# Two cached attention decodes on one core: the order of the first loads, and when the second problem's queries are made

## The chip, the cores and the metric

The kernel runs on one core of one Trainium2 chip. The metric is the device time of one execution in microseconds, the median of several runs. Five engines work side by side, each with an instruction stream of its own: TensorE (PE, with its weight loads shown apart as PEld), VectorE (DVE), ScalarE (ACT), GpSimd (POOL) and SyncE (SP). SP computes nothing here; it issues nearly all loads. Streams meet only at semaphores: an instruction waits until another engine, or a transfer that lands, has counted a semaphore up to a value. An engine that waits holds up everything behind it in its own stream.

## The reference

Two independent problems A and B of the same shape are computed, each one step of multi-head attention against a stored cache, and their results stand side by side:

```python
# B, Sq, D = 8, 1, 1024;  H, Sk, Dh = 32, 4096, 128;  bfloat16
q = (x @ wq).reshape(B, Sq, H, Dh).transpose(0, 2, 1, 3)
scores = einsum("bhqd,bhkd->bhqk", q, k_cache) * Dh ** -0.5
p = softmax(scores, axis=-1)
o = einsum("bhqk,bhkd->bhqd", p, v_cache)
result = o.transpose(0, 2, 1, 3).reshape(B, Sq, H * Dh) @ wo
```

Every batch row and head has keys and values of its own, 1 MB each, and they are used once. All of them have to come from memory: 2 x 2 x 8 x 32 MB and the weights.

## The kernel before, in words

**Slots.** The work is cut into 64 slots (`NS`), numbered n: problem c, group g of eight heads, batch row b. A slot's keys are one load of 8 MB (8.39 million bytes) into 128 partitions, 16 partitions to a head and 256 keys to a partition; its values are another of the same size. `kbuf` has two places for keys, used in turn (`k0`, `k1`); `vbuf` has one place for values (`v`). Below, K0, K1 and so on are the key loads, and V0, V1 and so on the value loads, of slots 0, 1 and so on.

**One slot.** `multiply` (line 354, DVE) multiplies a quarter of the keys with the slot's query in place, in `kbuf`; `add_up` (line 364, PE) sums the products over parts of the head dimension into the banks `red`; `reduce` (line 376, DVE) finishes the sums into the scores in `osb`. This happens four times, and the last `add_up` sets the key place free. `softmax` (lines 381 to 385, DVE) finds the maxima, `exps` (line 392, ACT) makes the eight heads' exponentials into `prob` and their row sums. `rowsum` (line 398, PE) and `invert` (line 404, DVE) make the reciprocals of the row sums. The product with the values, `pv` (line 415, PE), is done one slot later: slot n does `pv(n-1)` behind its last `add_up`, which sets `vbuf` free. `copy_o`, `gather` and `heads` bring the results into place; now and then `permute` and `project` multiply them with a part of the output weights, with `asb`, `osum` and `orow` as the places of the projection.

**Order.** `Program.add` records every operation with what it reads and writes by name, and puts it at the end of its engine's stream. `finish` turns these names into semaphore waits. A load into a place waits, on SP, for the last reader of that place. So the streams have exactly the order in which the Python code calls `add`. In slot n (line 542 on) the call order on SP is: `load_k(n)`, sometimes a load of output weights, `load_v(n-1)`. So V(n-1) and K(n+1) are issued right behind each other, when `pv(n-2)` is done in slot n-1. Slots from 1 on run in hardware loops on PE, ACT and DVE.

**The start.** Before slot 0 the queries are made. `load_wq` (line 251) loads the query weights of a problem, 8 MB like a key load: A's into `vbuf`, B's into the second key place, one behind the other. `make_xT` (line 257) transposes the inputs x, which ACT's queue has loaded, and puts them into a part of `prob` (`xT`). `make_q` (line 267) has three steps: 64 matmuls with 512 columns each (line 273, PE), in groups of four that stand side by side in the array, into the banks `oacc` and `late`; two casts to bfloat16 (line 278, DVE) into another part of `prob` (`qrow`); and 32 small matmuls that turn the rows into columns (line 284, PE), with a copy into `qT` (line 288, DVE). `pick_q(0)` (line 335, POOL) and `make_qbc(0)` (lines 342 and 346, PE and ACT) then spread the queries of slots 0 and 1 over the partitions, into `qbc`; they need A's queries alone. The sequence is A's weights, B's weights, K0 on SP without a wait; then K1, which goes into the place of B's weights and so waits for B's `make_q` matmuls; then V0, whose place A's matmuls have left.

Of the kernel before, what the change touches and what calls it, by code (L numbers as in the profile page):

```python
# [8 lines left out]
BF16 = mybir.dt.bfloat16  # L9
# [134 lines left out]
def _build(nc, caches, out):  # L144
    x0, k0, v0, wq0, wo0 = caches[0]
    B, Sq, D = x0.shape
    _, H, Sk, Dh = k0.shape
    NC = len(caches)
# [7 lines left out]
    R = D // 128  # L156
# [9 lines left out]
    with es:  # L166
# [8 lines left out]
        kbuf = sb("kbuf", [128, 2, T * Dh], BF16)  # L175
        vbuf = sb("vbuf", [128, T * Dh], BF16)
        wob = sb("wob", [128, 2, D], BF16)
        prob = sb("prob", [128, T, HP], BF16)
        osb = sb("osb", [128, TB * Dh], FP32)
        asb = sb("asb", [128, CW], FP32)  # L180
        osum = sb("osum", [128, CW], FP32)
        orow = sb("orow", [128, CW], BF16)
        qT = sb("qT", [128, NC, H * B], BF16)
        qbc = sb("qbc", [128, 2, Dh], BF16)
        ident = sb("ident", [128, 128], BF16)
# [15 lines left out]
        score = osb[:, 0:T]  # L201
        olate = asb[:, 0:2 * Dh]
        xs = wob[:].rearrange("p a n -> p (a n)").rearrange("p (c n) -> p c n", c=NC)
        flat = prob[:].rearrange("p t h -> p (t h)")
        xT = flat[:, 0:NC * R * B].rearrange("p (c r b) -> p c r b", c=NC, r=R)
        qrow = flat[:, 1024:2048].rearrange("p (k n) -> p k n", k=2)
        otail = kbuf[:, 1, 0:2 * TB * Dh].bitcast(FP32)
        wlast = vbuf[:, 0:HP * D].rearrange("p (h n) -> p h n", h=HP)

# [1 line left out]
        oacc = ps("oacc", [128, 512])  # L211
        late = ps("late", [128, 512])
        acc = ps("acc", [128, 512])
        bps = ps("bps", [128, 512])
        sps = ps("sps", [128, 512])
        qps = [(oacc, "oacc"), (late, "late")]
# [6 lines left out]
        def dma(eng, dst, src, writes, sem, reads=()):  # L223
            return P.add(eng, lambda e: e.dma_start(dst, src), reads=reads, writes=writes, dma=sem)  # L224
# [24 lines left out]
                op.sig = True  # L249

        def load_wq(c):
            dst = (vbuf[:], kbuf[:, 1, :])[c]
            name = ("v", "k1")[c]
            dma("sp", dst, caches[c][3].rearrange("(p r) n -> p (r n)", r=R), [name], name)
            return name, dst.rearrange("p (r n) -> p r n", r=R)

        def make_xT(c):
            def emit(e):
                last = None
                for r in range(R):  # L260
                    last = e.matmul(sps[:, 256 + r * B:256 + (r + 1) * B], xs[0:B, c, r::R], ident[0:B, 0:B], start=True, stop=True)
                return last
            P.add("pe", emit, reads=[f"xs{c}", "wo", "ident"], banks=["sps"])
            P.add("dve", lambda e: e.tensor_copy(xT[:, c].rearrange("p r b -> p (r b)"), sps[:, 256:256 + R * B]),
                  reads=probs, writes=[f"xT{c}"], banks=["sps"])

        def make_q(c, name, w):
            def emit(e):
                last = None
                for r in range(R):  # L270
                    for k in range(8):
                        q = k % 4
                        last = e.matmul(qps[k // 4][0][32 * q:32 * q + B, :], xT[:, c, r, :], w[:, r, k * 512:(k + 1) * 512],  # L273
                                        start=(r == 0), stop=(r == R - 1), tile_position=(0, 32 * q))
                return last
            P.add("pe", emit, reads=[name, f"xT{c}"] + probs, banks=["oacc", "late"])
            for k in range(2):
                P.add("dve", lambda e, k=k: e.tensor_copy(qrow[:, k, :], qps[k][0][:]), reads=probs, writes=[f"qrow{k}"], banks=[qps[k][1]])  # L278

            def turn(e):  # L280
                last = None
                for h in range(H):
                    q, k = (h // 4) % 4, h // 16
                    last = e.matmul(bps[:, h * B:(h + 1) * B], qrow[:, k, (h % 4) * Dh:(h % 4 + 1) * Dh],
                                    ident[:, 32 * q:32 * q + B], start=True, stop=True)
                return last
            P.add("pe", turn, reads=["qrow0", "qrow1", "ident"] + probs, banks=["bps"])
            P.add("dve", lambda e: e.tensor_copy(qT[:, c, :], bps[:, 0:H * B]), writes=[f"qT{c}"], banks=["bps"])

        def source(c, what, b, g):  # L290
# [7 lines left out]
        def load_k(n):  # L298
            c, g, b = where(n)
            dma("sp", kbuf[:, n % 2, :], source(c, 1, b, g), [f"k{n % 2}"], f"k{n % 2}")  # L300
# [31 lines left out]
        def pick_q(n):  # L332
            c, g, b = where(n)
            src = qT[:, c, g * HP * B:(g + 1) * HP * B].rearrange("p (h b) -> p b h", b=B)[:, b:b + 2, :]
            P.add("pool", lambda e: e.tensor_copy(qg[:], src.unsqueeze(3).to_broadcast([128, 2, HP, SEG])),
                  reads=[f"qT{c}"], writes=["qg"])

        def make_qbc(n):
            def emit(e):
                last = None  # L340
                for j in range(2):
                    last = e.matmul(bps[:, j * Dh:(j + 1) * Dh], qg[:, j].rearrange("p h s -> p (h s)"), ident[:],  # L342
                                    start=True, stop=True)
                return last
            P.add("pe", emit, reads=["qg", "ident"], banks=["bps"])
            P.add("act", lambda e: e.activation(qbc[:].rearrange("p i d -> p (i d)"), bps[:, 0:2 * Dh], ACTF.Copy),  # L346
                  writes=["qbc"], banks=["bps"])
# [31 lines left out]
        def softmax(n):  # L379
            i = n % 2  # L380
            P.add("dve", lambda e: e.tensor_reduce(rmax[:], score, AX.X, ALU.max), reads=scores, writes=["rmax"])  # L381
            P.add("dve", lambda e: e.transpose(tmax[:], rmax[:].to_broadcast([128, 32])), reads=["rmax"], writes=["tmax"])  # L382
            P.add("dve", lambda e: e.tensor_reduce(nmax[:], tmax[:].rearrange("p (s k) -> p s k", s=2), AX.X, ALU.max),
                  reads=["tmax"], writes=["nmax"])
            P.add("dve", lambda e: e.scalar_tensor_tensor(
                bias[:].rearrange("p (k s) -> p k s", s=2), nmax[:].unsqueeze(1).to_broadcast([128, HP // 2, 2]), -scale,
                neg[:].rearrange("p (k s) -> p k s", s=2), ALU.mult, ALU.add), reads=["nmax", "neg"], writes=["bias"])
# [139 lines left out]
        NS = NC * NG * B  # L527
        L0, L1, L2 = 1, B + 1, NS - 1
        vplace = {}
        first = [load_wq(c) for c in range(NC)]  # L530
        for c in range(NC):
            make_xT(c)
        for c, (name, w) in enumerate(first):
            make_q(c, name, w)
            if c == 0:
                pick_q(0)
                make_qbc(0)

        def marks():
            return {e: len(P.order[e]) for e in ("pe", "act", "dve")}  # L540
# [1 line left out]
        for n in range(NS):  # L542
            m = n - 1
            p = (n - B - 2) // 2 if n >= B + 2 and n % 2 == 0 else NP * (NC * NG - 1) - 1 if n == NS - 1 else None
            if n in (L1, L2):
                for e, at in marks().items():
                    P.loops[e].append((start[e], at, (n - was) // 2))
            if n in (L0, L1):
                start, was = marks(), n
            load_k(n)  # L550
            if p is not None:
                load_wo(p)
                pick_heads(p)
            if m >= 0:
                load_v(m)
            if n % 2 == 1 and n + 1 < NS:
                pick_q(n + 1)
            multiply(n, 0)
            if n >= 1:
                heads(n - 2)  # L560
                invert(n - 1)
            add_up(n, 0)
            multiply(n, 1)
            if p is not None:
                permute()
            reduce(n, 0)
            if p is not None:
                permuted()
            add_up(n, 1)
            multiply(n, 2)  # L570
            if p is not None:
                project()
            reduce(n, 1)
            add_up(n, 2)
            multiply(n, 3)
            reduce(n, 2)
            if p is not None:
                projected(p)
            add_up(n, 3)
            reduce(n, 3)  # L580
            softmax(n)
            if m >= 0:
                pv(m)
            if n % 2 == 1 and n + 1 < NS:
                make_qbc(n + 1)
            if n == NS - 1:
                load_v(n)
                load_wo_last()
            exps(n)
            if m >= 0:  # L590
                copy_o(m)
                if n == NS - 1:
                    idle(3)
                gather(m)
            if n == NS - 1:
                heads(m)
                idle(36)
            rowsum(n)
            if n == B * NG + B + 4:
                store(0)  # L600
# [112 lines left out]
```

## Time and profile before

| what | value |
|---|---|
| median of three runs | 2571.3 us (2571.07 to 2572.44) |
| span of the profiled execution | 2570.6 us |
| busy: PE | 1472.9 us (57%) |
| busy: DVE | 1372.3 us (53%) |
| busy: ACT | 647.2 us (25%) |
| busy: POOL | 314.9 us (12%) |
| SP's main DMA queue | 1107.33 MB, 99.8% of 16 engines' span |
| chain that ended last | DMA 33%, PE 23%, DVE 20%, unknown queue 13%, issue 9% |

How to read it. The shares of the engines are busy time over the span; the DMA row counts the time that the queue's packets took, as a share of the time of 16 DMA engines. The page divides the span into 40 slices of 64 us, and gives what the DMA moved in each. The chain is followed back from the last instruction, at each step to what released it. "Unknown queue" stands for waits that end with a landing that the profile does not put to a line. In a timeline each row has its start, its duration, engine, line, operation, and the tile written and read; in brackets the idle time of the engine just before it and what ended that. Queue rows (SPq) show when a load was issued; the time to landing is given apart.

### The profile page before, as it was taken

What the parts mean: (1) busy time and instruction counts of PE and PEld (TensorE: products, weight loads), DVE (VectorE), ACT (ScalarE), POOL (GpSimd) and SP (SyncE); (2) the same over time, 40 slices, a digit from 0 to 9 for tenths busy, and PEclk for the clock granted to TensorE, in tenths of its full rate; (3) what the DMA queues carried; (4) which work ended last, traced back from release to release, by engine and by line L of the source; (5) the groups of instructions that cost most, each with busy time, mean ns of one, the idle gap of its engine ahead of it and who ended that gap; (6) DMA issues with size and microseconds to landing.
All of it is one profiled execution on the core that took longest, in us unless ns stands there. A gap on an engine that the chain in (4) does not pass through costs nothing.

```text
span 2570.6 us, 19444 instructions
## 1 busy us (share of the span) xinstructions
PE 1472.9 (57%) x9528; PEld 290.3 (11%) x5688; DVE 1372.3 (53%) x969; ACT 647.2 (25%) x1121; POOL 314.9 (12%) x166
## 2 busy tenths in 40 slices
PE   2565565565555655655656656556555565565566
PEld 1011111011111111010111111110101111111102
DVE  1755465465564554645645545546456455465463
ACT  0223313313223123132132231331322322313313
POOL 0011011011011110110111101101101111011010
PEclk7877787877877878878778778787787787787888
DMA  9999999999999999999999999999999999999999
GB/s 424 393 439 426 440 433 435 432 430 432 432 433 432 436 434 432 432 432 428 440 433 432 432 432 430 432 432 435 435 432 434 432 433 433 432 435 432 432 432 391
DMA packets 24446, 1107.55 MB, mean 431 GB/s; under 512 B 2720, under 2 KB 2784, under 8 KB 7408
## 3 DMA queue, kind: packets, MB, share of 16 engines
q1 hardware_dynamic: 24368, 1107.33, 99.8%
q8 instruction: 8, 0.13, 0.0%
q10 hardware_dynamic: 64, 0.04, 0.0%
q14 instruction: 6, 0.05, 0.0%
HBM read 1107.33 MB, written 0.03 MB: 431 GB/s over the span
## 4 chain that ended last, share of the span: by engine, by line
DMA 33%; PE 23%; DVE 20%; another core or an unknown queue 13%; issue 9%; ACT 2%; SPq 0%; DVEq 0%; ACTq 0%
PE red L364 18%; DMA kbuf<-in_B_k_cache_dram 17%; DVE kbuf L354 16%; DMA kbuf<-in_A_k_cache_dram 13%; PE oacc L415 4%; DVE osb L376 3%; DMA kbuf<-in_B_wq_dram 2%; ACT prob L392 1%; DMA vbuf<-in_B_wo_dram 1%; SPq L224 0%; DVE on L457 0%; DVEq L646 0%; DVE rmax L381 0%; ACT qbc L346 0%
## 5 line engine op out<-in xcount | busy, mean ns | idle before, releaser
L354 DVE TENSOR_TENSOR kbuf<-kbuf,qbc 128x8192 bf16<-128x8192 bf16 x256 | 1128.3, 4408 | 784.8 <-DMA kbuf<-in_B_k_cache_dram 361.3
L364 PE MATMUL red<-kbuf,ident 128*128 128x512 bf16 x4096 | 1054.4, 418 | 399.0 <-DVE kbuf L354 206.7
L392 ACT ACTIVATE prob<-osb,bias 128x256 bf16<-128x256 f32 x512 | 598.7, 1583 | 947.1 <-PE oacc L415 892.5
L459 POOL COPY ona<-on 128x8 bf16<-128x8 bf16 x64 | 278.7, 4354 | 1859.9 <-DVE on L457 1859.9
L444 PE MATMUL sps<-sel,osb 128*128 128x8 f32 x504 | 115.4, 358 | 648.5 <-ACT osb L434 648.3
L376 DVE TENSOR_REDUCE osb<-red 128x64 f32<-128x512 f32 x256 | 176.0, 688 | 299.1 <-PE red L364 299.1
L392 ACT ACTIVATION_READ_ACCUMULATOR prob<-osb,bias 128x1 f32 x512 | 253.1, 494 | 0.0
L346 ACT ACTIVATE qbc<-bps 128x256 bf16<-128x256 f32 x32 | 12.3, 383 | 925.7 <-PE bps L342 925.7
L415 PE MATMUL oacc<-vbuf,prob 128*32 128x512 bf16 x4032 | 229.1, 380 | 0.0
L444 PEld LDWEIGHTS sps<-sel,osb 128*128 128x128 f32 x504 | 111.3, 325 | 667.9 <-issue 667.9
L415 PEld LDWEIGHTS oacc<-vbuf,prob 128*32 128x32 bf16 x4032 | 101.5, 97 | 315.5 <-issue 219.1
L364 PEld LDWEIGHTS red<-kbuf,ident 128*128 128x128 bf16 x256 | 25.4, 99 | 961.7 <-issue 939.8
L499 POOL TENSOR_TENSOR osum<-asb,osum 104x256 f32<-104x256 f32 x25 | 18.1, 723 | 308.5 <-DVE asb L493 308.5
L398 PE MATMUL sps<-rsum,ones 128*128 128x8 f32 x128 | 36.6, 359 | 11.4 <-ACT prob L392 11.3
L434 ACT ACTIVATE osb<-oacc 128x512 f32<-128x512 f32 x63 | 37.6, 597 | 10.8 <-PE oacc L415 3.8
L398 PEld LDWEIGHTS sps<-rsum,ones 128*128 128x128 f32 x128 | 34.7, 330 | 15.4 <-ACT prob L392 14.9
L381 DVE TENSOR_REDUCE rmax<-osb 128x1 f32<-128x256 f32 x64 | 26.9, 420 | 7.6
L470 PEld LDWEIGHTS sps<-ong,ident 128*64 128x64 bf16 x112 | 4.1, 109 | 153.2 <-issue 153.2
L278 DVE CAST prob<-oacc 128x512 bf16<-128x512 f32 x2 | 1.4, 691 | 35.6 <-PE late L273 35.6
L457 DVE TENSOR_TENSOR on<-sps,rl 128x8 bf16<-128x8 f32 x64 | 10.2, 159 | 16.9 <-PE sps L398 15.8
L382 DVE STREAM_TRANSPOSE tmax<-rmax 128x32 f32<-128x32 f32 x64 | 13.5, 212 | 7.7
L404 DVE RECIPROCAL rl<-sps 128x8 f32<-128x8 f32 x64 | 12.7, 198 | 8.0 <-PE sps L398 8.0
(61 smaller groups left out, 156.4 us busy)
## 6 DMA issues: line engine op xcount, KB each, us to landing
wob<-in_A_wo_dram SPq DMA_DIRECT2D x16, 512.0 KB, 51.1
wob<-in_B_wo_dram SPq DMA_DIRECT2D x12, 512.0 KB, 51.3
kbuf<-in_B_v_cache_dram SPq DMA_DIRECT2D x1, 4096.0 KB, 42.8
kbuf<-in_B_v_cache_dram SPq DMA_DIRECT2D x1, 2048.0 KB, 47.2
kbuf<-in_B_v_cache_dram SPq DMA_DIRECT2D x2, 1024.0 KB, 50.2
vbuf<-in_B_wo_dram SPq DMA_DIRECT2D x4, 512.0 KB, 15.4
kbuf<-in_A_k_cache_dram SPq DMA_DIRECT2D x32, 50.1
vbuf<-in_A_v_cache_dram SPq DMA_DIRECT2D x32, 31.3
```

Of the source, the lines that this page charges most:

```text
L354: P.add("dve", lambda e: e.tensor_tensor(kv, kv, qbc[:, n % 2, :].unsqueeze(1).to_broadcast([128, CT, Dh]), ALU.mult), reads=[f"k{n % 2}", ...
L364: first = e.matmul(rv, ident[:], pj[:, :, 0, :], start=True, stop=False).ins
L376: P.add("dve", lambda e: e.tensor_reduce(score[:, ch * CT:(ch + 1) * CT], rv, AX.X, ALU.add), writes=[f"score{ch}"], banks=[f"red{i}"])
L381: P.add("dve", lambda e: e.tensor_reduce(rmax[:], score, AX.X, ALU.max), reads=scores, writes=["rmax"])
L382: P.add("dve", lambda e: e.transpose(tmax[:], rmax[:].to_broadcast([128, 32])), reads=["rmax"], writes=["tmax"])
L392: P.add("act", lambda e, h=h: e.activation(prob[:, :, h], score, ACTF.Exp, bias=bias[:, h:h + 1], scale=scale, accum_out=rsum[:, i, h:h + 1]),
L398: P.add("pe", lambda e: e.matmul(sps[:, i * HP:(i + 1) * HP], ones[:].to_broadcast([128, 128]), rsum[:, i, :], start=True, stop=True), rea ...
L415: last = e.matmul(to[32 * q:32 * q + tb * HP, 0:tb * Dh], prob[:, t:t + tb, :].rearrange("p t h -> p (t h)"), buf[:, t * Dh:(t + tb) * Dh] ...
L434: P.add("act", lambda e: e.activation(osb[:], oacc[:], ACTF.Copy), writes=scores, banks=["oacc"])
L444: last = e.matmul(sps[:, o:o + HP], of[:, t * Dh:(t + 1) * Dh], sel[:, t, :], start=(t == 0 and not after), stop=(t == tb - 1 and (after o ...
L459: P.add("pool", lambda e: e.tensor_copy(ona[:, gi % 2, :, b], on[:, i, :]), reads=[f"on{i}"], writes=[f"ona{gi % 2}"])
L499: P.add("pool", lambda e: e.tensor_tensor(dst[0:104, :], asb[0:104, :], osum[0:104, :], ALU.add), reads=["asb", "osum"], writes=[name])
```

## The change

SP's first loads stand in another order: A's query weights into `vbuf`, K0, B's query weights, also into `vbuf`, K1. `load_wq` has one place for both problems. `load_wq(1)` is called behind A's `make_q`, `pick_q(0)` and `make_qbc(0)`, so it waits for A's matmuls, which read `vbuf`. K0 is called ahead of the main loop, and the loop calls `load_k` from slot 1 on. K1 goes into a place that nothing has used, so it waits for nothing itself, but stands behind B's weights on SP.

B's `make_q` is called inside slot 0, between `softmax(0)` and `exps(0)`: on PE it stands behind slot 0's last `add_up` and ahead of `rowsum(0)`, on DVE behind the maxima and ahead of slot 1. V0 waits for its matmuls, and K2 stands behind V0 on SP, whose own wait is then already met.

Since `prob` holds exponentials by then, the transposed inputs `xT` move to `orow`, and the two halves of `qrow` to `asb` and `osum`, read as bfloat16. The waits on `prob` go with that; both transposed inputs now have one name, `orow`.

```diff
-        flat = prob[:].rearrange("p t h -> p (t h)")
-        xT = flat[:, 0:NC * R * B].rearrange("p (c r b) -> p c r b", c=NC, r=R)
-        qrow = flat[:, 1024:2048].rearrange("p (k n) -> p k n", k=2)
+        xT = orow[:, 0:NC * R * B].rearrange("p (c r b) -> p c r b", c=NC, r=R)
+        qrow = [(asb[:].bitcast(BF16), "asb"), (osum[:].bitcast(BF16), "osum")]
...
         def load_wq(c):
-            dst = (vbuf[:], kbuf[:, 1, :])[c]
-            name = ("v", "k1")[c]
-            dma("sp", dst, caches[c][3].rearrange("(p r) n -> p (r n)", r=R), [name], name)
-            return name, dst.rearrange("p (r n) -> p r n", r=R)
+            dma("sp", vbuf[:], caches[c][3].rearrange("(p r) n -> p (r n)", r=R), ["v"], "v")
...
-            P.add("pe", emit, reads=[name, f"xT{c}"] + probs, banks=["oacc", "late"])
+            P.add("pe", emit, reads=["v", "orow"], banks=["oacc", "late"])
...
-        first = [load_wq(c) for c in range(NC)]
+        load_wq(0)
+        load_k(0)
         for c in range(NC):
             make_xT(c)
-        for c, (name, w) in enumerate(first):
-            make_q(c, name, w)
-            if c == 0:
-                pick_q(0)
-                make_qbc(0)
+        make_q(0)
+        pick_q(0)
+        make_qbc(0)
+        load_wq(1)
...
-            load_k(n)
+            if n >= 1:
+                load_k(n)
...
             softmax(n)
+            if n == 0:
+                make_q(1)
             if m >= 0:
                 pv(m)
```

More of the change, by code (lines that the diff above doesn't have):

```diff
@@ L264, in make_xT, with make_q @@
             P.add("dve", lambda e: e.tensor_copy(xT[:, c].rearrange("p r b -> p (r b)"), sps[:, 256:256 + R * B]),
-                  reads=probs, writes=[f"xT{c}"], banks=["sps"])
-        def make_q(c, name, w):
+                  writes=["orow"], banks=["sps"])
+        def make_q(c):
+            w = vbuf[:].rearrange("p (r n) -> p r n", r=R)
             def emit(e):
@@ L275, in emit @@
                 return last
-            P.add("pe", emit, reads=[name, f"xT{c}"] + probs, banks=["oacc", "late"])
+            P.add("pe", emit, reads=["v", "orow"], banks=["oacc", "late"])
             for k in range(2):
-                P.add("dve", lambda e, k=k: e.tensor_copy(qrow[:, k, :], qps[k][0][:]), reads=probs, writes=[f"qrow{k}"], banks=[qps[k][1]])
+                P.add("dve", lambda e, k=k: e.tensor_copy(qrow[k][0], qps[k][0][:]), writes=[qrow[k][1]], banks=[qps[k][1]])
             def turn(e):
@@ L283, in turn @@
                     q, k = (h // 4) % 4, h // 16
-                    last = e.matmul(bps[:, h * B:(h + 1) * B], qrow[:, k, (h % 4) * Dh:(h % 4 + 1) * Dh],
+                    last = e.matmul(bps[:, h * B:(h + 1) * B], qrow[k][0][:, (h % 4) * Dh:(h % 4 + 1) * Dh],
                                     ident[:, 32 * q:32 * q + B], start=True, stop=True)
                 return last
-            P.add("pe", turn, reads=["qrow0", "qrow1", "ident"] + probs, banks=["bps"])
+            P.add("pe", turn, reads=["asb", "osum", "ident"], banks=["bps"])
             P.add("dve", lambda e: e.tensor_copy(qT[:, c, :], bps[:, 0:H * B]), writes=[f"qT{c}"], banks=["bps"])
```

## The prediction

> **What bounds the kernel now.** I read the page first, for the load on the DMA engines; then the waits of the vector engine, for holes in the stream; then the load queue's timeline, and the time from issue to landing of each early load.
>
> ```profile
> span 2570.6 us, 19444 instructions
> DMA  9999999999999999999999999999999999999999
> GB/s 424 393 439 426 440 433 435 432 430 432 432 433 432 436 434 432 432 432 428 440 433 432 432 432 430 432 432 435 435 432 434 432 433 433 432 435 432 432 432 391
> HBM read 1107.33 MB, written 0.03 MB: 431 GB/s over the span
> ```
>
> The DMA engines carry the kernel: 1107 MB, and 428 to 440 GB/s in every slice but the first (424), the second (393: 64 to 128 us) and the last. No arithmetic can end it sooner; only time in which the stream stands still can be won back. The first product of a slot often waits for its K load, so its start dates the landing (the last column names the releaser):
>
> ```profile
> 62.72 8.76 DVE L354 TENSOR_TENSOR kbuf<-kbuf,qbc 128x8192 bf16<-128x8192 bf16 x2 [10.16 <-DMA kbuf<-in_A_k_cache_dram]
> ...
> 165.06 4.42 DVE L354 TENSOR_TENSOR kbuf<-kbuf,qbc 128x8192 bf16<-128x8192 bf16 x1 [7.18 <-DMA kbuf<-in_A_k_cache_dram]
> ...
> 242.55 4.43 DVE L354 TENSOR_TENSOR kbuf<-kbuf,qbc 128x8192 bf16<-128x8192 bf16 x1 [12.30 <-DMA kbuf<-in_A_k_cache_dram]
> ...
> 2522.06 4.42 DVE L354 TENSOR_TENSOR kbuf<-kbuf,qbc 128x8192 bf16<-128x8192 bf16 x1 [14.18 <-DMA kbuf<-in_B_k_cache_dram]
> ```
>
> These are slots 0, 3, 5 and 63. Between slots 3 and 5 lie four loads of 8.39 MB: 77.49/4 = **19.37 us a load**, 433 GB/s. Between slots 3 and 63 lie 120 such loads and 27 of output weights, a sixteenth as large: 120 x 19.37 + 27 x 1.21 = 2357.1, against 2357.0 in the rows. So from slot 3 to the end there is no hole. Between slots 0 and 3 lie five loads, 96.9 us, and the rows have 102.3: **5.5 us are lost there**, and only there. The queue shows where (start, duration; the third line holds two issues, the second of them just before 50.2):
>
> ```profile
> 0.74 0.41 SPq L224 DMA_DIRECT2D vbuf<-in_A_wq_dram  x1
> 1.21 0.42 SPq L224 DMA_DIRECT2D kbuf<-in_B_wq_dram  x1
> 1.67 48.51 SPq L224 DMA_DIRECT2D kbuf<-in_A_k_cache_dram  x2
> 50.22 0.44 SPq L224 DMA_DIRECT2D vbuf<-in_A_v_cache_dram  x1
> 87.39 0.33 SPq L224 DMA_DIRECT2D kbuf<-in_A_k_cache_dram  x1
> 122.44 0.33 SPq L224 DMA_DIRECT2D vbuf<-in_A_v_cache_dram  x1
> 122.82 0.43 SPq L224 DMA_DIRECT2D kbuf<-in_A_k_cache_dram  x1
> 159.25 0.33 SPq L224 DMA_DIRECT2D vbuf<-in_A_v_cache_dram  x1
> ```
>
> Their times to landing (last number), in the order A's weights, B's weights, K0, K1, V0, K2, V1, K3:
>
> ```profile
> vbuf<-in_A_wq_dram SPq DMA_DIRECT2D x1, 21.9
> kbuf<-in_B_wq_dram SPq DMA_DIRECT2D x1, 42.1
> kbuf<-in_A_k_cache_dram SPq DMA_DIRECT2D x1, 61.0
> kbuf<-in_A_k_cache_dram SPq DMA_DIRECT2D x1, 32.2
> vbuf<-in_A_v_cache_dram SPq DMA_DIRECT2D x1, 51.2
> kbuf<-in_A_k_cache_dram SPq DMA_DIRECT2D x1, 33.3
> vbuf<-in_A_v_cache_dram SPq DMA_DIRECT2D x1, 22.5
> kbuf<-in_A_k_cache_dram SPq DMA_DIRECT2D x1, 42.1
> ```
>
> Issue plus time gives landings at 22.6, 43.3, 62.7, 82.0, 101.4, 120.7, 144.9 and 164.9. They come in the order of issue, one load apart, with one exception: V1 lands 24.2 us behind K2, and K3 20.0 behind V1. That is 4.9 + 0.6 = 5.5, the loss above. V1 was issued at 122.44, when K2 had landed: slot 1 finished that late, because it starts only when slot 0 is through (K2's issue at 87.39 waited for slot 0's last sum), and slot 0 could not start before the third load landed at 62.7. The stretches show the stream dry (columns: span; busy PE, PEld, DVE, ACT, POOL; clock, DMA share, GB/s; a packet counts where it starts):
>
> ```profile
> 116.00:116.25 0.25, 0.25 (x3) 0.00 (x0) 0.00 (x0) 0.00 (x0) 0.00 (x0) 1.00 4.85 2097
> 117.75:118.00 0.25, 0.25 (x3) 0.00 (x0) 0.00 (x0) 0.00 (x0) 0.00 (x0) 1.00 1.21 524
> 118.00:123.00 5.00, 4.57 (x70) 1.72 (x66) 1.68 (x5) 0.32 (x2) 0.00 (x0) 1.00 0.00 0
> 123.25:123.50 0.25, 0.00 (x0) 0.00 (x0) 0.23 (x1) 0.25 (x1) 0.00 (x0) 1.00 5.52 1835
> ```
>
> From 118 to 123 us no packet starts. A packet takes 2.4 us (share over rate: 4.85 x 0.25 us x 16 engines = 19.4 engine-us for 2097 x 0.25 = 524 KB, eight packets of 64 KB). Most engines are done at 118.6, 2.1 us ahead of K2's landing, and V1's first packets come 0.8 us after its issue. So a load keeps the stream whole if it is **issued 2.9 us before its predecessor lands**.
>
> **The change, part by part.** Nothing is removed: the same loads, matmuls and copies run, so the bytes stay. What moves is order.
>
> First, K0 takes second place and B's weights third, into the V buffer. K0 then lands at 43.3 instead of 62.7. B's weights wait for A's query matmuls to leave the V buffer, and K1 stands behind that wait. Those matmuls begin at 22.6 and last as long as B's do now:
>
> ```profile
> 43.39 0.60 PE L273 MATMUL oacc<-kbuf,prob 128*8 128x512 bf16 x4 [10.53 <-DMA kbuf<-in_B_wq_dram]
> ...
> 48.89 0.42 PE L273 MATMUL late<-kbuf,prob 128*8 128x512 bf16 x4
> 49.14 0.39 PE L273 MATMUL oacc<-kbuf,prob 128*8 128x512 bf16 x4
> 49.36 0.39 PE L273 MATMUL late<-kbuf,prob 128*8 128x512 bf16 x4
> 49.80 0.69 DVE L278 CAST prob<-oacc 128x512 bf16<-128x512 f32 x1 [17.85 <-PE late L273]
> ...
> 52.14 0.42 DVE L288 CAST qT<-bps 128x256 bf16<-128x256 f32 x1 [1.05 <-PE bps L284]
> ```
>
> From 43.39 to 49.75 are 6.4 us; so B's weights are issued at 29.0 and K1 at 29.5. The limit is 43.3 - 2.9 = 40.4: cost nothing, cover 11 us. They land at 62.7 and 82.0 as their places do now.
>
> Second, slot 0's sums. Now they take from 62.72 to K2's release at 87.39, 24.7 us. From 43.3 on they end at 68.0, and B's weights have landed by then.
>
> Third, B's queries behind them. Sixteen groups of four matmuls cost 6.4 us as measured; at the pace of the last groups (49.14 to 49.36, 0.22 apart) 16 x 0.22 + 0.2 = 3.7. I take 6.4, the dearer: they end at 74.4. V0 waits for them, and K2, whose buffer was free at 68.0, stands behind V0 on SP: both go out at 74.4 to 75.3. K1 lands at 82.0, limit 79.1: cost nothing, cover 4.7 us (7.4 by the lower price). Casts, turn and copy end at 52.56 now, 2.8 us behind the matmuls, so at 77.2 then. Queued behind them on DVE are slot 1's products, which need K1 at 82.0 anyway; on PE slot 0's row sum. Nothing is paid. The new homes of xT and qrow (orow, asb, osum) are idle until the first projection. A's queries now name the same tile as B's transposed inputs, and so wait for a cast at 11 us, long past at 22.6.
>
> Fourth, slot 1 starts at 82.0 with K1. A settled slot, from its K landing to the next V issue:
>
> ```profile
> 242.55 4.43 DVE L354 TENSOR_TENSOR kbuf<-kbuf,qbc 128x8192 bf16<-128x8192 bf16 x1 [12.30 <-DMA kbuf<-in_A_k_cache_dram]
> ...
> 269.79 0.33 SPq L224 DMA_DIRECT2D vbuf<-in_A_v_cache_dram  x1
> ```
>
> 27.2 us. Slots 1 and 2 are longer now:
>
> ```profile
> 89.19 1.43 ACT L392 ACTIVATE prob<-osb,bias 128x256 bf16<-128x256 f32 x1 [54.57 <-DVE bias L385]
> ...
> 98.09 0.50 ACT L392 ACTIVATION_READ_ACCUMULATOR prob<-osb,bias 128x1 f32 x1
> ...
> 89.62 4.43 DVE L354 TENSOR_TENSOR kbuf<-kbuf,qbc 128x8192 bf16<-128x8192 bf16 x1 [0.46 <-issue]
> ...
> 123.28 4.43 DVE L354 TENSOR_TENSOR kbuf<-kbuf,qbc 128x8192 bf16<-128x8192 bf16 x1 [2.20 <-ACT qbc L346]
> ```
>
> Slot 1 goes from 89.62 to V1's issue, 32.8 us, slot 2 from 123.28 to V2's, 36.0. Both start together with the exponentials of the slot before, 9.4 us (89.19 to 98.59), and DVE's second step needs their sums. Begun at 82.0, slot 1 has those of slot 0 behind it: 1.8 us after the sums (87.39 to 89.19), 69.8 to 79.2. So V1 and K3 go out between 109.2 and 114.8, by the two lengths. K2 lands at 120.7 as now, limit 117.8: the hole closes with 3 to 8.6 us to spare. Slot 2 starts at 120.7, at least 5 us into slot 1's exponentials, and issues V2 at 147.9, or with slot 1's 32.8 at 153.5; K3 lands at 159.4, limit 156.5. Only its own present 36.0 would miss that, by 0.2. From there a slot of 27.2 has 38.7 us of loads to hide under.
>
> **The sum.** 4.9 us of dry stream and 0.6 of slow restart go, and nothing is added: span 2570.6 - 5.5 = 2565.1. The median of the runs stands 0.7 above the profiled span, so **2571.3 - 5.5 = 2565.8 us**. The end of the kernel hangs on the stream too and shifts with it.
>
> **Rivals.**
>
> *The hole is worth less.* The slowest engine started its last K2 packet before 118.0, was done at 120.4 and stood still until 123.4; if only its 3.0 us and the restart's 0.6 count, the time is 2567.7, and with the 4.9 alone 2566.4. Against it, the landings, which the slowest engine sets, are a steady 19.3 to 19.4 apart before the hole. [...]
>
> *More comes.* B's weights land 20.7 us behind A's, 1.4 over a load. If that belongs to this load and not to the start, K0 in its place saves it: 2564.4. The second landing carries the start's lag whatever is loaded, so I doubt it.
>
> *Slower: V0 comes too late.* The one new chain is K0, sums, B's queries, V0. If K0 did not land ahead of B's weights but with them, at 62.7 (loads sharing the engines), the sums would end at 87.4, the queries at 91.1 to 93.8, and V0 be 12.0 to 14.7 us past its limit of 79.1. With the restart's 0.6 and the old hole gone, the time is 2571.3 - 5.5 + 12.6 to 15.3 = 2578.4 to 2581.1. It decides from V0's issue at 84.0. Three loads queued within 1.7 us landed one by one, which speaks against it.
>
> *The hole moves to V2.* If slot 2 keeps 36.0 us from 120.7, V2 misses by 0.2 and the restart costs 0.6: 2566.6. At 40.7 us the whole gain is gone and the change does nothing for the time: 2571.3. The exponentials, which made it long, then come earlier, which speaks against it.
>
> **How the numbers follow.** Forecast 0.68, hole worth less 0.14, more 0.06, hole at V2 0.06, slower 0.06. The range goes from the larger gain to the smaller, 2564.4 to 2567.7, and leaves out slower and the far end of the hole at V2. About 0.2% (5.1 us, to 2566.2) can be told from no change; the forecast is 0.4 us beyond it and the three runs scatter by 1.4, so about three quarters of its chance count as faster: 0.51, with 0.06 of more and 0.05 of the first rival 0.62. Same is 0.17 + 0.09 + 0.06 = 0.32, slower 0.06.
>
> **What would show it.** Right: products of slot 0 at 43, V0's issue at 72 to 75, of slot 1 at 82, V1's issue before 115, the second slice near 432 GB/s, V1's landing 19.4 behind K2's, slot 3's first product at 159.5. Wrong: packets missing around 80 or 118 us, or a landing over 20 us behind its predecessor.

## The result, and the profile after

The changed kernel takes 2566.98 us (median of 20 runs, 2566.78 to 2567.99), the kernel before 2571.41 us (20 runs, 2569.98 to 2572.79). The ratio is 0.9983, 95% interval 0.9977 to 0.9990: 4.4 us less, clear of noise, though less than the 0.2% that the prediction took as its bound, and 1.2 us short of the forecast of 2565.8. The profiled span went from 2570.6 to 2565.0 us, where 2565.1 had been worked out. So the trace and the times disagree by about a microsecond, and that is the main question of the experiments.

First the page of the changed kernel, as shown of before:

```profile
span 2565.0 us, 19446 instructions
GB/s 425 430 436 432 434 434 432 434 432 433 433 433 431 432 433 433 433 433 433 433 433 433 433 432 434 433 432 432 433 429 439 433 433 432 432 430 432 433 433 392
HBM read 1107.33 MB, written 0.03 MB: 432 GB/s over the span
```

The bytes are the same. The second slice, 393 GB/s before, now moves 430; the first and the last are as they were. The load queue's timeline of the changed kernel (start, duration):

```profile
1.21 0.42 SPq L223 DMA_DIRECT2D kbuf<-in_A_k_cache_dram  x1
28.51 0.33 SPq L223 DMA_DIRECT2D vbuf<-in_B_wq_dram  x1
28.89 0.43 SPq L223 DMA_DIRECT2D kbuf<-in_A_k_cache_dram  x1
70.21 0.33 SPq L223 DMA_DIRECT2D vbuf<-in_A_v_cache_dram  x1
70.59 0.43 SPq L223 DMA_DIRECT2D kbuf<-in_A_k_cache_dram  x1
110.24 0.33 SPq L223 DMA_DIRECT2D vbuf<-in_A_v_cache_dram  x1
110.62 0.44 SPq L223 DMA_DIRECT2D kbuf<-in_A_k_cache_dram  x1
```

The times to landing of the last five of these, K1, V0, K2, V1, K3:

```profile
kbuf<-in_A_k_cache_dram SPq DMA_DIRECT2D x1, 53.1
vbuf<-in_A_v_cache_dram SPq DMA_DIRECT2D x1, 31.1
kbuf<-in_A_k_cache_dram SPq DMA_DIRECT2D x1, 50.1
vbuf<-in_A_v_cache_dram SPq DMA_DIRECT2D x1, 29.8
kbuf<-in_A_k_cache_dram SPq DMA_DIRECT2D x1, 48.9
```

They land at 82.0, 101.3, 120.7, 140.0 and 159.5: one load apart throughout, and V1 no longer 24.2 us behind K2. V1 goes out at 110.24, 10.4 us before K2 lands; before, it went out 1.7 us after. The vector engine's first products of slots 0, 1, 2 and 3:

```profile
43.26 8.76 DVE L352 TENSOR_TENSOR kbuf<-kbuf,qbc 128x8192 bf16<-128x8192 bf16 x2 [12.05 <-DMA kbuf<-in_A_k_cache_dram]
...
82.08 4.43 DVE L352 TENSOR_TENSOR kbuf<-kbuf,qbc 128x8192 bf16<-128x8192 bf16 x1 [9.14 <-DMA kbuf<-in_A_k_cache_dram]
...
120.78 4.43 DVE L352 TENSOR_TENSOR kbuf<-kbuf,qbc 128x8192 bf16<-128x8192 bf16 x1 [11.91 <-DMA kbuf<-in_A_k_cache_dram]
...
159.67 4.43 DVE L352 TENSOR_TENSOR kbuf<-kbuf,qbc 128x8192 bf16<-128x8192 bf16 x1 [12.67 <-DMA kbuf<-in_A_k_cache_dram]
```

All four now wait for their K load; before, slots 1 and 2 did not. Slot 3 starts 5.4 us earlier than before (165.06), and the span is 5.6 shorter: the gain is made by then and kept to the end. B's queries cost their low price (the first and the last group of matmuls):

```profile
66.50 0.39 PE L271 MATMUL oacc<-vbuf,orow 128*8 128x512 bf16 x4
...
69.73 0.39 PE L271 MATMUL late<-vbuf,orow 128*8 128x512 bf16 x4
```

From 66.50 to the end of the last group at 70.12 are 3.6 us, 0.22 a group.

For each run both its time and the span of the same execution are known. In the changed kernel the time stands 1.76 to 2.4 us above the span. The profiled execution of before had a span of 2570.6, while the median time then at hand was 2571.3, 0.7 above. If the same 1.8 holds there, that execution was one of the longer ones.

### The profile page after: what moved, and what is told of

Read it like the earlier page. It is cut to its first block, busy times and chain, and to the rows that moved or that the text cites. A ratio compares the mean times of both kernels' runs of the same rounds, so it can differ in the third digit from the quotient of the medians.

```text
span 2565.0 us, 19446 instructions
## 1 busy us (share of the span) xinstructions
PE 1472.9 (57%) x9528; PEld 290.1 (11%) x5688; DVE 1371.9 (53%) x969; ACT 647.2 (25%) x1121; POOL 314.9 (12%) x166
## 4 chain that ended last, share of the span: by engine, by line
DMA 40%; PE 22%; DVE 18%; another core or an unknown queue 9%; issue 9%; ACT 1%; SPq 0%; DVEq 0%; ACTq 0%
DMA kbuf<-in_A_k_cache_dram 21%; DMA kbuf<-in_B_k_cache_dram 19%; PE red L362 16%; DVE kbuf L352 14%; PE oacc L413 5%; DVE osb L374 2%; ACT prob L390 1%; PE red L516 0%; SPq L223 0%; DVE on L455 0%; DVEq L647 0%; DVE rmax L379 0%; ACT qbc L344 0%; DVE rl L402 0%
## 5 line engine op out<-in xcount | busy, mean ns | idle before, releaser
L333 POOL COPY qg<-qT 128x256 bf16<-128x256 bf16 x32 | 12.7, 396 | 28.0 <-DVE qT L286 27.5
L381 DVE TENSOR_REDUCE nmax<-tmax 128x2 f32<-128x32 f32 x64 | 11.9, 186 | 7.6
```

## The experiments

### The kernel of before, profiled again

No edit.

> The kernel of before, unchanged, profiled again. Theory 'varying hole': device time stands 1.8 us above the span in every run of either kernel (1.76 to 2.4 in the twenty of the changed one), so before's spread of times (2570.0 to 2572.8) is a spread of spans, 2568.2 to 2571.0, and the one profiled execution (2570.6) was a long one. Its hole between K2 and V1 differs from run to run, with V1's issue. Then the new profile has span = 2565.1 + (landing V1 - landing K2 - 19.37) + 0.6, whatever the span is, and V1's issue moves by as much as the span. Rival 'constant offset': before's time is 0.8 us above its span and the changed kernel's 1.9; the spans of before then stand at 2569.2 to 2572.0, and the hole stays 5.5 us in every run.

Measured: 2571.37 us (11 runs), ratio 1.0000 (0.9991 to 1.0009). In its 11 runs and in 28 more of the kernel before, the time stands 1.75 to 2.0 us above the span, a few times up to 2.9; the spans go from 2568.4 to 2570.8, median 2569.35 of the 28. The profiled execution has a span of 2569.6. Its queue rows for K2 and V1, and below the clock of TensorE (third number from the end) in three stretches, first of this execution, then of the one shown in the prediction:

```profile
86.54 0.33 SPq L224 DMA_DIRECT2D kbuf<-in_A_k_cache_dram  x1
121.22 0.33 SPq L224 DMA_DIRECT2D vbuf<-in_A_v_cache_dram  x1
```

```profile
70.00:72.00 2.00, 2.00 (x8) 0.00 (x0) 1.35 (x1) 0.00 (x0) 0.00 (x0) 0.68 1.21 524
72.00:74.00 2.00, 2.00 (x11) 0.10 (x1) 1.17 (x2) 0.00 (x0) 0.00 (x0) 1.00 1.18 500
102.00:104.00 2.00, 2.00 (x10) 0.10 (x1) 1.31 (x2) 0.00 (x0) 1.25 (x1) 1.00 0.38 164
```

```profile
70.00:72.00 2.00, 2.00 (x7) 0.00 (x0) 1.48 (x1) 0.00 (x0) 0.00 (x0) 0.50 1.21 524
72.00:74.00 2.00, 2.00 (x9) 0.10 (x1) 0.33 (x1) 0.00 (x0) 0.00 (x0) 0.79 1.18 500
102.00:104.00 2.00, 2.00 (x7) 0.00 (x0) 2.00 (x1) 0.00 (x0) 2.00 (x1) 0.61 0.30 131
```

The clock reached full speed earlier here, in slot 0's sums and again in slot 1's. K2 went out 0.85 us sooner (86.54 against 87.39), V1 1.2 us sooner (121.22 against 122.44), and the span is 1.0 shorter. V1 landed 22.8 us behind K2, not 24.2; by the formula of the expectation that makes 2569.1, 0.5 short of the measured 2569.6. The rival's constant 0.8 us is out: the spans show that the offset is the same for both kernels. The hole itself differs from run to run.

### Keeping TensorE busy in the kernel of before

```diff
+        idle(60)
+
         def marks():
...
+            if n == 0:
+                idle(46)
             rowsum(n)
```

`idle(k)` issues k matmuls of the identity into a bank that nothing reads at that time.

> Before, with 60 idle matmuls ahead of slot 0's first sum and 46 ahead of slot 0's row sum, so that PE does not stand idle there and its clock stays up. Order of loads and queries as before. Theory 'varying hole': the first sums of slots 0 and 1 take 3.6 us instead of 5.7, slot 0 ends about 2 us earlier and slot 1 about 3, V1 is issued near 119.3 instead of 122.4, and the hole shrinks to 2.4 us with the restart: time 2569.3 (2568.6 to 2570.0), spread of the runs under 1 us. Rival 'the loss has nothing to do with when slots 0 and 1 end': time 2571.4, spread 2.8.

Measured: 2569.54 us (11 runs), ratio 0.9992 (0.9983 to 1.0001); the interval just reaches no change. The profiled span is 2567.0, and V1 goes out at 118.75. The median fits the theory; the spread does not: spans from 2566.7 to 2569.1, 2.4 us wide where under 1 was expected. Two more executions of the same kernel were profiled for that.

> A second profile of the kernel with the idle matmuls, whose runs went on to spread by 2.3 us. Theory 'clock phase': where its span is above 2567.5, the trace shows a stretch of half clock in the idle blocks or in slots 0 and 1 that the first profile (span 2567.0) does not have, and V1 is issued later than 118.75 by as much as the span is longer. Rival 'the stream itself varies': V1's issue is the same and the loads land further apart.

> The same once more, for another execution: theory 'clock phase' and rival 'the stream itself varies' as for the last one; the span is 2565.0 + (V1's issue - 117.8) + 1.0 by the first, and free of V1's issue by the second.

Measured: spans 2568.9 and 2566.7. Here are the first idle block, slot 0's first sums and the issue of V1, then the clock in slot 0's and in slot 1's sums, in the first profile of this kernel:

```profile
51.45 14.79 PE L518 MATMUL red<-ident 128*128 128x512 bf16 x60
67.17 3.61 PE L364 MATMUL red<-kbuf,ident 128*128 128x512 bf16 x16 [0.93 <-DVE kbuf L354]
...
118.75 0.33 SPq L224 DMA_DIRECT2D vbuf<-in_A_v_cache_dram  x1
```

```profile
68.00:70.00 2.00, 2.00 (x11) 0.00 (x0) 2.00 (x1) 0.00 (x0) 0.00 (x0) 1.00 0.30 131
...
98.00:100.00 2.00, 2.00 (x11) 0.00 (x0) 2.00 (x1) 0.00 (x0) 2.00 (x1) 1.00 1.21 524
```

and in the second:

```profile
50.91 13.11 PE L518 MATMUL red<-ident 128*128 128x512 bf16 x60
67.12 8.75 PE L364 MATMUL red<-kbuf,ident 128*128 128x512 bf16 x32 [3.10 <-DVE kbuf L354]
...
120.82 0.33 SPq L224 DMA_DIRECT2D vbuf<-in_A_v_cache_dram  x1
```

```profile
68.00:70.00 2.00, 2.00 (x6) 0.00 (x0) 2.00 (x1) 0.00 (x0) 0.00 (x0) 0.50 0.38 164
...
98.00:100.00 2.00, 1.96 (x6) 0.10 (x1) 1.90 (x3) 0.00 (x0) 1.68 (x1) 0.55 1.21 524
```

In the first, a stretch at half clock (0.50 from 52 to 54 us) made the idle block longer (14.8 us), so it reached close to the first sums, 0.9 us ahead, and these ran at full clock (1.00 from 68 to 70 us). In the second the block ran at full speed (1.00 from 52 to 64 us), ended early after 13.1 us, and TensorE then stood idle for 3.1 us; the clock fell to half just as the sums began (0.87 from 66 to 68 us, 0.50 from 68 to 70), and K2 went out 1.2 us later (86.17 against 84.98). In slot 1 it fell again, at 98.2 us (0.55 from 98 to 100, 1.00 in the first), though the idle time ahead of the row sum was 1.5 us in both executions; this is the rest of V1's delay. V1 went out 2.1 us later (120.82 against 118.75), and the span is 1.9 longer; the formula of the last expectation gives 2569.0. The third execution is like the first (V1 at 118.94, span 2566.7, formula 2567.1). The rival, a stream that varies, is out: the span follows V1's issue. The idle matmuls did not hold the clock in every run.

### The order alone

Before, with the loads in the new order, but B's weights in the second key place and B's queries ahead of slot 0:

```diff
-        first = [load_wq(c) for c in range(NC)]
+        first = [load_wq(0)]
+        load_k(0)
+        first.append(load_wq(1))
...
-            load_k(n)
+            if n >= 1:
+                load_k(n)
```

> Before, with only the order of loads changed: A's weights, K0, B's weights (second key place), K1; B's queries stay ahead of slot 0 on PE and DVE. Theory: slot 0 waits for B's queries, whose weights land at 62.7: queries done at 71.9, sums at 96.6, V1 issued at about 129.8, 12 us past its limit of 117.8; time 2567.0 + 12.0 + 0.6 = 2579.6 (2577 to 2581), slower than before by 8. Rival 'K0's early landing alone brings the gain': 2567 to 2568.

Measured: 2580.79 us (5 runs), ratio 1.0035 (1.0021 to 1.0048), span 2579.1. The size is as expected, the place is half wrong. The rows of K1 and V1:

```profile
69.01 0.33 SPq L224 DMA_DIRECT2D kbuf<-in_A_k_cache_dram  x1
...
131.15 0.33 SPq L224 DMA_DIRECT2D vbuf<-in_A_v_cache_dram  x1
```

There are two holes. K1 waits for B's matmuls in its place, and goes out 6.2 us after B's weights have landed (1.67 + 61.1 = 62.8); no load is left by then. K2 then lands at 131.0, and V1 goes out 0.2 us later, for a second hole. The expectation had seen only V1, 12 us late. V1 is late because slot 0's first product stands behind B's queries on DVE: it begins at 71.6 us, though K0 landed at 43.3. So K0's early landing brings nothing by itself: slot 0 must not stand behind B's queries. The other half alone, B's queries behind slot 0's sums with the loads in the old order, was not run.

### V0 made late on purpose

The changed kernel, with idle matmuls ahead of B's queries; 56 of them, and in a second kernel 28:

```diff
             if n == 0:
+                idle(56)
                 make_q(1)
```

> The changed kernel with 56 idle matmuls between slot 0's last sum and B's query matmuls, so that V0 and K2 are issued 12.1 us later, at 82.3 instead of 70.2. Theory: V0's limit is 79.1 (2.9 before K1's landing), so the stream stands 3.2 us and loses 0.6 at the restart: V0 lands 23.2 behind K1, V1 in time; time 2567.0 + 3.8 = 2570.8 (2570.3 to 2571.3). Rival 'only the slowest engine's idle counts': 2567.0 + 1.3 to 2.1 = 2568.3 to 2569.1. [...]

Measured: 2571.65 us (11 runs), 4.7 us above the changed kernel, span 2569.5. V0's issue, and its time to landing:

```profile
82.69 0.33 SPq L223 DMA_DIRECT2D vbuf<-in_A_v_cache_dram  x1
```

```profile
vbuf<-in_A_v_cache_dram SPq DMA_DIRECT2D x1, 21.8
```

V0 went out 0.4 us behind K1's landing (29.11 + 53.2 = 82.3), 0.4 later than planned, and the span is 4.5 longer. The theory's 3.8 is too small, and the rival, with 1.3 to 2.1, is further off.

> The changed kernel with 28 idle matmuls between slot 0's last sum and B's query matmuls, so that V0 and K2 are issued 6.0 us later, at about 76.3, inside the cover (limit 79.1, cover then 2.8 us). Theory: no hole, V0 lands 19.4 behind K1, time 2567.0 (2566.7 to 2567.5), and the runs stay as close together as those of the changed kernel (within 1.3 us). Rival 'any delay of V0 costs', as a stream that is issued late starts late: 2567.0 + 6 = 2573, or a part of it in proportion.

Measured: 2567.33 us (11 runs, 2566.81 to 2568.69), span 2565.2, V0 issued at 76.41. Its row and time to landing:

```profile
76.41 0.33 SPq L223 DMA_DIRECT2D vbuf<-in_A_v_cache_dram  x1
```

```profile
vbuf<-in_A_v_cache_dram SPq DMA_DIRECT2D x1, 24.8
```

V0 lands at 101.2, 19.4 us behind K1 (81.85). The time and the profile agree with the theory and rule out a price for delay as such. The spread does not agree: 1.9 us, where 1.3 was expected, since three runs have spans of 2566.5 to 2566.8. They may be those in which the clock made slot 0 long and V0 missed its limit. No such execution was profiled, so this stays open.

### B's weights in the second key place

The changed kernel, but:

```diff
-            dma("sp", vbuf[:], caches[c][3].rearrange("(p r) n -> p (r n)", r=R), ["v"], "v")
+            dst, name = ((vbuf[:], "v"), (kbuf[:, 1, :], "k1"))[c]
+            dma("sp", dst, caches[c][3].rearrange("(p r) n -> p (r n)", r=R), [name], name)
...
-            P.add("pe", emit, reads=["v", "orow"], banks=["oacc", "late"])
+            P.add("pe", emit, reads=[name, "orow"], banks=["oacc", "late"])
```

> The changed kernel with B's weights in the second key place, as before, not in the V buffer: order of loads and the place of B's queries are those of the changed kernel. Then K1, not V0, waits for B's query matmuls, behind slot 0's sums. Theory: K1 is issued near 70.2, its limit is 59.8 (2.9 before B's weights land at 62.7), a hole of 10.4 and about 1.0 at the restart, as the five holes so far cost 0.8 to 1.2 beyond the lateness: time 2567.0 + 11.4 = 2578.4 (2577 to 2580). Rival 'the place does not matter, order and deferral do': 2567.

Measured: 2579.34 us (6 runs), ratio 1.0032 (1.0020 to 1.0044), span 2576.2. K1:

```profile
70.11 0.33 SPq L223 DMA_DIRECT2D kbuf<-in_A_k_cache_dram  x1
```

It goes out 7.4 us after B's weights have landed (62.7). So the place is a part of the change that counts: with B's weights in the V buffer, the load that must wait for them is V0, one load later.

### All holes in one table

Loss is the span over 2565.0; the lateness is the issue of the load less the landing of the one ahead of it in the stream, in the same profile.

| kernel | load | lateness, us | loss, us | loss - lateness |
|---|---|---|---|---|
| before, first profile | V1 | 1.75 | 5.6 | 3.85 |
| before, again | V1 | 0.4 | 4.6 | 4.2 |
| before, idle matmuls | V1 | -1.9 | 2.0 | 3.9 |
| the same, second | V1 | 0.15 | 3.9 | 3.75 |
| the same, third | V1 | -1.8 | 1.7 | 3.5 |
| order alone | K1 and V1 | 6.2 + 0.2 | 14.1 | 7.7 for two |
| 56 idle matmuls | V0 | 0.4 | 4.5 | 4.1 |
| B's weights in k1 | K1 | 7.4 | 11.2 | 3.8 |
| 28 idle matmuls | V0 | -5.4 | 0.2 | none |

By these rows, a load issued later than about 3.9 us (3.5 to 4.2) ahead of its predecessor's landing costs the kernel a microsecond for each microsecond. Issued 5.4 us ahead, it cost nothing clear.

## Why the prediction was right, and where it was wrong

**The hole between K2 and V1** as the only loss that the change can reach: right. Closing it took 5.6 us off the profiled span (5.5 expected), and longer or shorter holes, at three different loads, changed the span by as much.

**Bytes, order and places.** K0 at 43.3 (measured 43.26), slot 1 at 82.0 (82.08), V1 between 109.2 and 114.8 (110.24), slot 3 at 159.5 (159.67): right. Slot 0's sums took 23.3 us instead of 24.7 (43.26 to 66.57); the difference lies in the first two sums, 8.5 us instead of 9.8, as the clock came back sooner (0.81 from 50 to 52 us, 2.2 to 4.2 us into them; before, 0.50 from 70 to 72, 2.7 to 4.7 us into them).

**B's queries.** I took the dearer price, 6.4 us; they took 3.6, since TensorE comes to them from slot 0's sums at full clock (1.00 from 66 to 70 us; before, 0.50 from 44 to 48). V0 went out at 70.21, ahead of the 72 to 75 given as a sign. Nothing hung on it, as the cover was 4.7 us at the dearer price.

**The limit.** "Issued 2.9 us before its predecessor lands", with 0.6 for the restart, is 3.5 in all; the table has 3.9, and what the other 0.4 us are is not shown. The decision did not hang on it either.

**The step that was mis-sized** is in the sum: "The median of the runs stands 0.7 above the profiled span, so 2571.3 - 5.5". Both kernels stand 1.8 above their spans; the 0.7 compared one long execution with the median of others (of the 28 spans of before listed with the second profile, only three are longer than its 2570.6). The hole of 5.5 us belonged to that execution. In those 28 runs the spans of before have a median of 2569.35, so the usual hole costs 2569.35 - 2565.15 = 4.2 us, with 2565.15 the median span of the changed kernel. The times say 4.4. The time fell into the range (2564.4 to 2567.7), and the direction was right, but with the hole at its usual size the forecast belonged inside 0.2%: the 0.62 for a larger gain was on the wrong side. I had also taken the scatter of the three runs (1.4 us) for noise of the measurement. The changed kernel's runs span 1.2 us, and 15 of the 20 lie within 0.35; most of before's scatter was the hole.

**The rivals.** "The hole is worth less" gave 2566.4 to 2567.7, and the time lies there by luck, for another reason than its own: the trace shows the hole worth its whole length, and even a little more. "More comes" is out: K0 in second place lands 20.5 us behind A's weights (22.7 to 43.2), as B's did (20.7); the lag belongs to the start. "V0 comes too late" did not happen, but its price was right in kind: made late by hand, V0 cost 4.5 us of span, where that price makes 82.69 - 79.1 + 0.6 = 4.2. "The hole moves to V2" is out: V2 went out at 148.37, 11.1 us before K3 landed.

## What to carry to other kernels

In a kernel bound by one stream of loads, look for the first load that is issued too late to join the stream, ask which compute it waits for, and move work so that this compute starts earlier. Where every load still went out in time, slower compute cost little here: 28 idle matmuls cost 0.2 us of span. A load that has to wait should be the one with the most loads still queued ahead of it: the same weights in the other buffer cost 12 us here. Compare a kernel's time with its own span before subtracting a piece of one profile from a median, and where the runs scatter, ask whether the piece itself is what varies.

## What the runs showed of the hardware that was not expected

The time of this kernel, bound by loads, hung on TensorE's clock. At the same place in slot 0's sums the clock came back to full before 72 us in one execution of the kernel before and after it in another (0.68 against 0.50 from 70 to 72 us), and likewise in slot 1's sums (1.00 against 0.61 from 102 to 104). The first two sums took 9.08 us against 9.79 in slot 0 and 8.86 against 9.20 in slot 1; this made nearly all of the 1.2 us by which V1's issue moved, and the span moved by 1.0. How long TensorE had been idle does not decide it alone: with the idle matmuls, after the same 1.5 us ahead of slot 1's row sum, the clock fell in one execution (0.55 from 98 to 100 us) and held in two (1.00). In the one where it fell, the clock rose at 47.0, fell at 67.5, rose at 70.9, fell at 98.2 and rose at 101.6 us. What sets these times is not shown. The 28 spans of before differ by up to 2.4 us. In the changed kernel a late sum delays loads that have time in hand (V1 goes out 10.4 us before K2 lands), and 15 of its 20 runs lie within 0.35 us.
